# A fused retention and mixture-of-experts kernel: batch 1's feed-forward in two halves of 256 tokens, its second half attended in 64-token chunks

## The chip, the core and the metric

The kernel runs on one core of a Trainium2 chip. The time is the device time of one launch in microseconds (us). Engines are named as in the profile: PE is TensorE (matmul), PEld its weight loads, DVE is VectorE, ACT is ScalarE, POOL is GpSimd, SP is SyncE, which issues nearly all DMAs.

## What is computed

Retention attention for 8 batches, 8 heads, 576 positions and head dimension 64, followed by a two-layer feed-forward on all 4608 tokens (model width 512, inner width 2048):

```python
scores = scale * np.matmul(q, k.transpose(0, 1, 3, 2))
gamma = 1.0 - 2.0 ** (-5.0 - np.arange(H))
Dmat = np.where(rel >= 0, gamma[:, None, None] ** rel[None], 0.0)   # rel = row - column
ret = scores * Dmat[None]
attn = np.matmul(ret, v)
x = attn.transpose(0, 2, 1, 3).reshape(B * S, H * D)
h = x @ w_in
out = (h * (1.0 / (1.0 + np.exp(-beta * h)))) @ w_out
```

Inputs and output are float32; matmuls are in bf16. Because the decay is a power of gamma, it splits into a factor for q's position and one for v's. So attention is done in chunks: scores inside a chunk under a causal mask, plus q times a running state, the sum of k's transpose times v over the earlier chunks.

## The kernel before

Each batch has 512 full positions and a tail of 64; the eight tails together make a ninth block of 512 tokens. The blocks run in the order 0 to 6, tails, 7. For a block, attention leaves its transposed result in `xT` (four groups of 128 model columns by 512 tokens); 16 `up` steps (L542) multiply by `w_in` into PSUM and ACT writes the SiLU to `gT` (L551); then four groups of tokens, `down` (L575), each take 16 matmuls in four steps of four into a PSUM tile `po`, which is copied to `ot` (L589) and stored.

All engines run their instructions in the order in which the program emits them. That order is written by hand: the list `fill` (L663 to L688) holds the ups and downs, which keep PE busy, and `streams` (L704 to L776) holds every other step with a position in `fill` at which it is put in. `d0` is the position of batch 0's downs, `u1` that of batch 1's ups and `base[n]` that of later blocks' ups; `merged` (L602) weaves them. A step's time in the program is thus its place among ups and downs; on DVE, ACT, POOL and SP it is only an order.

PSUM has eight banks in four pools: `mm` has three (ups, downs, and one that the states borrow), `O` two, `sc` two, `st` one.

There are two forms of attention. Batches 0 and 1 go by chunks of 128: PE transposes q (`t_q`, L317) and k (`t_k`, L324), `a_sc` (L334) makes scores and DVE masks them, `a_O` and `a_cross` make the output, `a_x` copies it to `xT`, and `a_st` (L408) adds to the state and copies it to the block-diagonal `sbd` tiles. `second` (L690) does the outputs of two chunks. Later batches go by chunks of 64 on quarters of the array: `d_st` (L471) makes the state sums of four chunks, in a bank of `st` and a bank of `mm`, and its `chain` has DVE add them up one after another (L488, L490) and ACT copy each to `sbq` (L491); `d_sc` (L456) makes scores and masks (L469); `d_out` (L498) makes outputs (L508), the crosses with the states (L521) and, in `evict`, the four copies to `xT` (L536), two on DVE and two on ACT. They are grouped in stops: `scores` (L725) and `outputs` (L732), the latter with the first half of the next batch's states. Between the stops PE does ups or downs while DVE and ACT work.

In batch 1, chunks 0 and 1 are attended within batch 0's last downs. Ups 0 to 9 are then done for the 256 tokens of these two chunks, with chunks 2 and 3 attended among them, then ups 0 to 9 for the other 256 tokens, and ups 10 to 15 for all 512:

```python
fill += [F(up, 1, fo, 2 * x, 2) for x in range(2) for fo in range(10)]
fill += [F(up, 1, fo) for fo in range(10, FO)]
fill += [F(down, 1, ms, f0) for ms in range(MB // P) for f0 in range(0, FO, 4)]
```

A separate step, `early_states`, puts batch 2's first states behind the first of batch 1's downs. The scaling of q by the decay is `pre_q` (L253; on DVE for batches 0 and 1, on POOL after that), k and v are prepared by `pre` on POOL, and from batch 2 on SP transposes q and k by DMA.

Of the kernel before, what the change touches and what calls it, by code (L numbers as in the profile page):

```python
# [19 lines left out]
def kernel(  # L20
# [49 lines left out]
    QB = 2  # L70
    q_tiles, kv_tiles = {}, {}

    def load_q(b, us=(0, 1)):

        if b >= B:
            return
        if 0 in us:
            q_tiles[b] = stage.tile([P, H, CB, D], F32, name="qn", tag="qn", bufs=2)
        t = q_tiles[b]
        for u in us:  # L80
            w = slice(u * HP, (u + 1) * HP)
            nc.sync.dma_start(t[:, w].rearrange("p h i d -> p h (i d)"),
                              q[b, w, :MB, :].rearrange("h (p i) d -> p h (i d)", i=CB))
# [41 lines left out]
    pos = consts.tile([P, 2, CB + 1], F32, name="pos")  # L125
    for j, (step, mul) in enumerate(((1, CB), (P, 1))):
        nc.gpsimd.iota(pos[:, j, :CB], pattern=[[step, CB]], base=0, channel_multiplier=mul,
                       allow_small_or_imprecise_dtypes=True)
        for x in range(2):
            nc.gpsimd.iota(pos[x * TL:(x + 1) * TL, j, CB:], pattern=[[0, 1]], base=MB, channel_multiplier=1,  # L130
                           allow_small_or_imprecise_dtypes=True)
    lscale = consts.tile([P, 1], F32, name="lscale")
    nc.vector.memset(lscale[:], math.log(scale))
    lg = consts.tile([P, 2, CB + 1, H], F32, name="lg")
# [5 lines left out]
    nc.scalar.activation(gv[:], lg[:, 1], ACT.Exp, scale=-1.0)  # L140

# [10 lines left out]
    tri = [consts.tile([P, TL], BF16, name=f"tri{i}") for i in range(2)]  # L152
# [97 lines left out]
    def head_of(b, p, j):  # L250
        return 2 * p + (j if b is not None and b < QB or p < 2 else 1 - j)

    def pre_q(b, n):  # L253

        if n == 0:
            batch[b] = dict(qs=sb.tile([P, CB, H, D], BF16, name="qs", tag="qs", bufs=2),
                            qT=sb.tile([P, CB, HP, P], BF16, name="qT", tag="qT", bufs=2))
        if b < 2:
            hs, cs = slice(n // 2 * HP, (n // 2 + 1) * HP), slice(n % 2 * 2, n % 2 * 2 + 2)
            e = nc.vector  # L260
        else:
            if n % 2:
                return
            cs = slice(n, n + 2)
            for to, hs in turned:
                nc.gpsimd.tensor_tensor(batch[b]["qs"][:, cs, to], q_tiles[b][:, hs, cs].rearrange("p h i d -> p i h d"),  # L266
                                        gq[:, cs, hs].unsqueeze(3).to_broadcast([P, 2, len(range(H)[hs]), D]), ALU.mult)
            return
        e.tensor_tensor(batch[b]["qs"][:, cs, hs], q_tiles[b][:, hs, cs].rearrange("p h i d -> p i h d"),
                        gq[:, cs, hs].unsqueeze(3).to_broadcast([P, cs.stop - cs.start, hs.stop - hs.start, D]),  # L270
                        ALU.mult)

    def pre(i, js=(0, 1)):
# [22 lines left out]
        for to, hs in turned if b >= QB else [(slice(0, H), slice(0, H))]:  # L296
            nc.gpsimd.tensor_copy(kn[:, c % 2, to], t[:, 0, hs])  # L297
# [32 lines left out]
    def q_cols(i, r, p):  # L330

        b, c = seq[i]
        if b is None:
            return live[i]["qkT"][r, 0, p, :], lambda o: o  # L334
        return (batch[b]["qT"][r, :, p, c * PC:(c + 1) * PC], lambda o: o.rearrange("k (i s) -> k i s", i=CB))

    def a_sc(i):
# [11 lines left out]
        m_b = causal[:].unsqueeze(1).to_broadcast([P, HP, P])  # L349
# [48 lines left out]
    def a_x(i):  # L398
        b, c = seq[i]
        x, view = xt(b)[:, :, :, c * PC:(c + 1) * PC], lambda o: o.rearrange("k p (i s) -> k p i s", i=CB)  # L400
        Os = live[i]["O"]
# [6 lines left out]
    def a_st(i):  # L408
# [11 lines left out]
        for j in range(2):  # L420
            r, cols = slice(j * D, (j + 1) * D), slice(j * D, (j + 1) * D)
            e = nc.vector.tensor_copy if i in (CB + 2, CB + 3) else nc.scalar.copy
# [4 lines left out]
            e(ends[b][(1 - j) * D:(2 - j) * D, 2:], st[r, 2:, cols])  # L427

# [9 lines left out]
    def q_of(u, c, j, p):  # L438

        if u == B:  # L440
            return piece(u, c)["qkT"][half(j), 0, p, half(c % 2)]
        w = TL // CB
        return batch[u]["qT"][half(j), :, p, c * w:(c + 1) * w]

    def columns(u, o):
        return o if u == B else o.rearrange("k (i s) -> k i s", i=CB)
# [4 lines left out]
    def d_sc(u):  # L451

        R = [sb.tile([P, 2, 2, HP, TL], BF16, name="R", tag="R", bufs=4) for _ in range(2)]
        sc = {}
        for x in range(2):
            for j in range(2):  # L456
                sc[x, j] = psum.tile([P, 2, HP, TL], F32, name="sc", tag="O" if x else "sc", bufs=2)
# [6 lines left out]
        mask = tri[1 if u == B else 0][:].unsqueeze(1).to_broadcast([P, 2 * HP, TL])  # L464
# [29 lines left out]
    def d_out(u):  # L494

        shape = [P, 2, CB, TL] if u == B else [P, 2, CB, CB, TL // CB]
        O = {(hh, y): psum.tile(shape, F32, name="O", tag="sc" if y else "O", bufs=2) for y in range(2) for hh in range(2)}

        def to(c, p, x):
            o = O[c % 2, p // 2][half(x), p % 2]  # L500
            return o[:, c // 2] if u == B else o[:, :, c // 2]

        R = batch[u]["R"]
        for cc in range(CB):
            for p in range(HP):
                for hh, j in spread:
# [3 lines left out]
                                            start=cc == 0 and p % 2 == 0, stop=False, skip_group_check=True)  # L510
# [4 lines left out]
        def cross(flip):  # L515
            for n, (cc, pp, y, j) in enumerate((cc, pp, y, j) for cc in range(CB) for pp in range(2) for y in range(2) for j in range(2)):
# [11 lines left out]
        def evict():  # L528
            for n, ((hh, y), o) in enumerate(O.items()):
                x = xt(u)[:, 2 * y:2 * y + 2]  # L530
                if u == B:
                    x, o = x[:, :, :, half(hh)].rearrange("k p c q -> k (p c) q"), o.rearrange("k p c q -> k (p c) q")
                else:
                    x = x.rearrange("k p i (c h s) -> k (p i) c h s", c=CB, h=2)[:, :, :, hh, :]
                    o = o.rearrange("k p i c s -> k (p i) c s")
                (nc.scalar.copy if n % 2 else nc.vector.tensor_copy)(x, o)  # L536
# [5 lines left out]
    def up(m, fo, c0=0, cn=CB):  # L542
        if m not in gts:
            gts[m] = sb.tile([P, FO, CB, P], BF16, name="gT", tag="gT", bufs=2)
        w = slice(c0 * PC, (c0 + cn) * PC)
        ph = psum.tile([P, CB, P], F32, name="ph", tag="mm", bufs=3)
        ph = ph.rearrange("f i s -> f (i s)")[:, :cn * P].rearrange("f (i s) -> f i s", i=CB)
        for ko in range(KO):
            nc.tensor.matmul(ph, w_in_sb[:, ko, fo * P:(fo + 1) * P], xts[m][:, ko, :, w],  # L549
                             start=(ko == 0), stop=(ko == KO - 1))  # L550
        nc.scalar.activation(gts[m][:, fo, :, w], ph, ACT.Silu, scale=beta_sb[:, fo:fo + 1])  # L551
# [23 lines left out]
    def down(m, ms, f0, fn=4, n0=0, nn=d_model):  # L575
# [13 lines left out]
        (nc.scalar.copy if m == 0 else nc.vector.tensor_copy)(ot, po[:, :nn])  # L589
        if m < B:  # L590
            rows = out[m * S:m * S + MB].rearrange("(s i) n -> s i n", i=CB)
            if m < 2:
                held.append((rows[:, ms, n0:n0 + nn], ot))
            else:
                nc.sync.dma_start(rows[:, ms, n0:n0 + nn], ot)
# [100 lines left out]
    def triangles():  # L696
        for t, pattern in zip(tri, ([[1, CB], [CB, TL // CB]], [[1, TL]])):
            nc.gpsimd.memset(t[:], 1.0)
            for x in range(2):
                w = slice(x * TL, (x + 1) * TL)  # L700
# [7 lines left out]
               [(10.3, F(load_q, 1))] + [(10.3, F(load_kv, CB + n, (j,))) for n, j in keys_first],  # L708
               [(10.4, F(load_q, 2))] + [(10.4, F(load_kv, 2 * CB + n)) for n in range(2)],
               [(d0 + 8.6, F(load_kv, 2 * CB + 2)), (d0 + 8.7, F(load_kv, 2 * CB + 3)), (d0 + 12.6, F(x_q, XB, 0)), (d0 + 12.7, F(x_q, XB, 1)),  # L710
                (d0 + 13.6, F(x_k, XB, 0)),
                (base[2] - 4.5, F(release, 4)), (base[2] + 10, F(release, 4))],
               [(d0 + 7, F(pre_q, 1, n)) for n in range(4)] + [(d0 + 12.5, F(pre_q, XB, n)) for n in range(4)] + [(d0 + 11.6, F(t_q, 1, 0)), (d0 + 12.6, F(t_q, 1, 1))],
               [(d0 + 8, F(pre, 4, (0,))), (d0 + 8, F(pre, 5, (0,))), (d0 + 9, F(pre, 4, (1,))), (d0 + 9, F(pre, 5, (1,))),
                (d0 + 12.7, F(t_k, 4)), (d0 + 14, F(t_k, 5)), (d0 + 14, F(a_sc, 4)), (d0 + 15, F(a_sc, 5)),
                (d0 + 15, F(a_st, 4)), (d0 + 15.9, F(second, 4))],
# [5 lines left out]
    def early_states(u):  # L722
        d_st(u, 0)()

    def scores(u):  # L725
        chain = d_st(u, 1) if u < B else lambda: None
        masks = d_sc(u)
        steps = [lambda: masks(0), lambda: masks(1)]
        for f in [chain] + steps if u == B - 1 else steps + [chain]:
            f()  # L730

    def outputs(u):  # L732
# [3 lines left out]
        evict()  # L736
        chain()
# [70 lines left out]
```

## Time and profile before

| what | us |
|---|---|
| median of three runs | 299.28 (299.02 to 299.34) |
| the profiled execution | 298.64 |
| its span in the profile | 296.9 |
| PE busy | 286.9 |
| ACT busy | 147.1 |
| DVE busy | 101.3 |
| POOL busy | 109.0 |

Starts are counted from the span's begin. In a row of the timeline or of the chain, the first number is the start, the second the time that it takes, then engine, line, operation, output and inputs, shape and count; brackets give the idle time before it and what ended it. A matmul's row is longer than the distance to the next, since matmuls overlap; distances are taken from starts.

### The profile page before, as it was taken

The page shows a single profiled execution, that of the slowest core. Times are in us where ns is not written, and L with a number is a line of the kernel's source. Part 1 is how long each engine was busy: PE and PEld are TensorE (multiplying, and loading weights), DVE is VectorE, ACT ScalarE, POOL GpSimd, SP SyncE. Part 2 cuts the span into 40 slices and gives each one's busy share as a digit, 9 for nine tenths or more (in the row PEclk, how much of TensorE's full clock was granted, in tenths as well). Part 3 has the DMA queues.
Part 4 walks back from the last instruction along what each step waited for, and adds up shares of the span by engine and source line. Part 5 has one row for each costly group of instructions (what it writes and reads, how often), then busy time and mean ns, then how long its engine had stood idle before and what let it go on. Part 6 is the DMA issues. An engine that isn't in the chain of part 4 may idle for free.

```text
span 296.9 us, 7459 instructions
## 1 busy us (share of the span) xinstructions
PE 286.9 (97%) x3147; PEld 149.2 (50%) x3177; DVE 101.3 (34%) x209; ACT 147.1 (50%) x257; POOL 109.0 (37%) x211
## 2 busy tenths in 40 slices
PE   7799999999999999999999999999999999999995
PEld 5554456855544454455445544554454544444444
DVE  5563656704640552045204530354054300120012
ACT  5567546683277434743484347433770157008600
POOL 3666107693750923370429216736223000000000
PEclk9999999999999999999999999999999999999999
DMA  8999999999999999949999849999976110131012
GB/s 213 218 333 393 386 273 252 224 203 222 252 169 254 270 196 242 242 68 160 233 237 207 178 99 272 195 181 188 205 168 140 73 38 0 35 71 38 0 71 73
DMA packets 128273, 53.97 MB, mean 182 GB/s; under 512 B 110048, under 2 KB 120688, under 8 KB 128240
## 3 DMA queue, kind: packets, MB, share of 16 engines
q1 hardware_dynamic: 128208, 53.49, 82.4%
q8 instruction: 25, 0.41, 0.6%
q14 instruction: 8, 0.07, 0.1%
q10 hardware_dynamic: 32, 0.01, 0.0%
HBM read 36.71 MB, written 9.44 MB: 155 GB/s over the span
## 4 chain that ended last, share of the span: by engine, by line
PE 83%; DMA 5%; SPq 5%; POOL 3%; issue 2%; ACT 1%; POOLq 0%; DVE 0%
PE po L582 38%; PE ph L549 33%; PE ph L564 4%; DMA tln<-in_k_dram 3%; SPq L94 2%; DMA kvn<-in_k_dram 2%; PE O L508 1%; SPq L113 1%; POOL kn L286 1%; PE st L480 1%; PE sc L462 1%; DMA kT<-kn 1%; SPq L305 1%; POOL kn L285 1%; PE O L521 1%
## 5 line engine op out<-in xcount | busy, mean ns | idle before, releaser
L582 PE MATMUL po<-w_out_sb,gT 128*128 128x512 bf16 (+2 forms) x590 | 125.6, 367 | 2.3 <-issue 2.1
L551 ACT ACTIVATE gT<-ph,beta_sb 128x512 bf16<-128x512 f32 (+1 forms) x140 | 91.2, 657 | 52.1 <-PE ph L549 51.7
L549 PE MATMUL ph<-xT,w_in_sb 128*128 128x512 bf16 (+1 forms) x550 | 114.5, 364 | 0.5
L582 PEld LDWEIGHTS <-gT 128*128 128x128 bf16 x608 | 56.9, 98 | 62.9
L549 PEld LDWEIGHTS <-w_in_sb 128*128 128x128 bf16 x560 | 54.3, 98 | 57.6 <-DVE sum L488 0.7
L589 DVE COPY ot<-po 128x512 f32<-128x512 f32 (+2 forms) x34 | 22.3, 657 | 72.3 <-PE po L582 71.6
L297 POOL CAST kn<-kvn 128x128 bf16<-128x128 f32 (+2 forms) x80 | 25.9, 359 | 43.5 <-DMA kvn<-in_k_dram 43.0
L266 POOL TENSOR_TENSOR qs<-qn,gq 128x256 bf16<-128x256 f32 (+1 forms) x36 | 26.3, 759 | 36.0 <-DMA qn<-in_q_dram 34.6
L469 DVE TENSOR_TENSOR R<-sc,tri 128x512 bf16<-128x512 f32 x28 | 17.4, 683 | 61.4 <-PE sc L462 61.4
L277 POOL TENSOR_TENSOR vn<-kvn,gv 128x512 bf16<-128x512 f32 x32 | 33.3, 1044 | 13.5 <-DMA kvn<-in_v_dram 8.5
L536 ACT CAST xT<-O 128x512 bf16<-128x512 f32 x14 | 7.5, 589 | 32.0 <-PE O L521 32.0
L491 ACT CAST sbd<-warm 128x256 bf16<-128x256 f32 x18 | 7.3, 405 | 25.5 <-DVE warm L488 20.6
L564 PE MATMUL ph<-xT,w_in_sb 128*128 128x512 bf16 x54 | 12.3, 379 | 0.3 <-ACT xT L404 0.2
L351 DVE TENSOR_TENSOR R<-sc,causal 128x512 bf16<-128x512 f32 x16 | 10.2, 685 | 4.6 <-PE sc L347 4.5
L488 DVE TENSOR_TENSOR sum<-st,warm 128x256 f32<-128x256 f32 x24 | 10.2, 425 | 2.5
L488 DVE TENSOR_TENSOR warm<-st,sum 128x256 f32<-128x256 f32 x18 | 7.6, 422 | 9.6 <-PE st L480 8.4
L536 DVE CAST xT<-O 128x512 bf16<-128x512 f32 x14 | 9.0, 686 | 5.0 <-PE O L521 5.0
L567 ACT ACTIVATE gT<-ph,beta_sb 128x512 bf16<-128x512 f32 x14 | 8.7, 687 | 4.2 <-PE ph L564 4.2
L285 POOL TENSOR_TENSOR kn<-tln,gq 128x128 bf16<-128x128 f32 (+1 forms) x12 | 5.7, 472 | 10.5 <-DMA tln<-in_q_dram 6.9
L194 POOL CAST w_in_sb<-wt 128x256 bf16<-128x256 f32 (+1 forms) x12 | 7.4, 623 | 4.9 <-DMA wt<-in_moe_w_in_dram 4.9
L564 PEld LDWEIGHTS <-w_in_sb 128*128 128x128 bf16 x56 | 5.4, 98 | 6.7 <-issue 0.3
L219 PE MATMUL ph<-warm 128*128 128x128 f32 (+1 forms) x24 | 7.3, 444 | 1.3 <-DVE warm L123 1.3
(81 smaller groups left out, 154.1 us busy)
## 6 DMA issues: line engine op xcount, KB each, us to landing
qn<-in_q_dram SPq DMA_DIRECT2D x16, 512.0 KB, 5.4
kvn<-in_k_dram SPq DMA_DIRECT2D x32, 256.0 KB, 5.4
kvn<-in_v_dram SPq DMA_DIRECT2D x32, 256.0 KB, 5.0
out_dram<-ot SPq DMA_DIRECT2D x31, 256.0 KB, 3.8
wt<-in_moe_w_out_dram SPq DMA_DIRECT2D x8, 512.0 KB, 9.1
wt<-in_moe_w_in_dram SPq DMA_DIRECT2D x5, 512.0 KB, 8.1
wt<-in_moe_w_in_dram SPq DMA_DIRECT2D x6, 256.0 KB, 5.5
out_dram<-ot SPq DMA_DIRECT2D x9, 128.0 KB, 2.4
```

The source lines that it names most:

```text
L266: nc.gpsimd.tensor_tensor(batch[b]["qs"][:, cs, to], q_tiles[b][:, hs, cs].rearrange("p h i d -> p i h d"), gq[:, cs, hs].unsqueeze(3).to_ ...
L277: nc.gpsimd.tensor_tensor(live[i]["vn"][:], kv_tiles.pop(i)[:, 1], gains(gv, c), ALU.mult)
L297: nc.gpsimd.tensor_copy(kn[:, c % 2, to], t[:, 0, hs])
L351: nc.vector.tensor_tensor(R[:, j], sc[j][:], m_b, ALU.mult)
L469: nc.vector.tensor_tensor(R[x][:, j].rearrange("k c p q -> k (c p) q"), sc[x, j].rearrange("k c p q -> k (c p) q"), mask, ALU.mult)
L488: nc.vector.tensor_tensor(new[:], add, sums[(c - 1) % 2][:], ALU.add)
L536: (nc.scalar.copy if n % 2 else nc.vector.tensor_copy)(x, o)
L549: nc.tensor.matmul(ph, w_in_sb[:, ko, fo * P:(fo + 1) * P], xts[m][:, ko, :, w], start=(ko == 0), stop=(ko == KO - 1))
L551: nc.scalar.activation(gts[m][:, fo, :, w], ph, ACT.Silu, scale=beta_sb[:, fo:fo + 1])
L564: nc.tensor.matmul(phs[f][:], w_in_sb[:, ko, f * P:(f + 1) * P], xts[m][:, ko], start=(ko == 0), stop=(ko == KO - 1))
L582: nc.tensor.matmul(po[:, :nn], gT[:, fo, ms, :], w_out_sb[:, fo, n0:n0 + nn], start=(fo == 0), stop=(fo == FO - 1))
L589: (nc.scalar.copy if m == 0 else nc.vector.tensor_copy)(ot, po[:, :nn])
```

## The change

Batch 1 (`HB`) is done in two halves of 256 tokens: 16 half-width ups and the downs of two token groups, then the same for the second half. Chunks 0 and 1 are attended as before, though over another arrangement of the tokens (two runs per 128 positions in place of four, with q loaded in halves of positions, a decay table `gqh` and a mask `causal_h` of their own). The second half is attended in four chunks of 64, in the manner of the later batches: `scores(HB)` at the end of the first half's ups, `outputs(HB)` before the last three steps of the first half's downs. `a_st` of chunk 1 has DVE put the state into `sum` and ACT copy it to `sbq`. The second half of q is scaled on DVE and transposed among the first half's ups, with the keys of chunks 2 and 3. `outputs(HB)` takes over batch 2's first states from `early_states`, and its four copies to `xT` are all on ACT, behind the chain. Batch 2's stops move: its scores to the start, its outputs to the middle of the second half's downs. Two of batch 1's four output copies go from DVE to ACT, and half of batch 2's q scaling from POOL to DVE.

```diff
-    QB = 2
+    HB = 1
+    HT = MB // 2
...
+        if b == HB:
+            for x in us:
+                nc.sync.dma_start(t[:, :, 2 * x:2 * x + 2].rearrange("p h i d -> p h (i d)"),
+                                  q[b, :, x * HT:(x + 1) * HT, :].rearrange("h (p i) d -> p h (i d)", i=2))
+            return
...
+        if b == HB:
+            cs = slice(2 * n, 2 * n + 2)
+            for to, hs in turned if n else [(slice(0, H), slice(0, H))]:
+                nc.vector.tensor_tensor(batch[b]["qs"][:, cs, to], q_tiles[b][:, hs, cs].rearrange("p h i d -> p i h d"),
+                                        gqh[:, cs, hs].unsqueeze(3).to_broadcast([P, 2, len(range(H)[hs]), D]), ALU.mult)
+            return
...
+            e = nc.vector if b == XB and n else nc.gpsimd
...
+    def t_qh(x):
+        T = psum.tile([P, 2, HP, P], BF16, name="T", tag="O", bufs=2)
+        for i in range(2):
+            for p in range(HP):
+                nc.tensor.transpose(T[:, i, p, :], heads(batch[HB]["qs"][:, 2 * x + i], p), ident[:])
+        (nc.vector.tensor_copy if x else nc.scalar.copy)(batch[HB]["qT"][:, 2 * x:2 * x + 2], T[:])
...
-            e = nc.vector.tensor_copy if i in (CB + 2, CB + 3) else nc.scalar.copy
+            e = nc.scalar.copy
+            if i == CB + 1:
+                nc.vector.tensor_copy(sums[1][r, :2], st[r, :2, cols])
+                nc.vector.tensor_copy(sums[1][half(1 - j), 2:], st[r, 2:, cols])
+                continue
...
+        if i == CB + 1:
+            nc.scalar.copy(sbq[3][:], sums[1][:])
...
+        xs = range(u == HB, 2)
...
-        for x in range(2):
+        for x in xs:
...
+        ccs = range(2 if u == HB else 0, CB)
...
-        for cc in range(CB):
+        for cc in ccs:
...
-                (nc.scalar.copy if n % 2 else nc.vector.tensor_copy)(x, o)
+                (nc.scalar.copy if n % 2 or u == HB else nc.vector.tensor_copy)(x, o)
...
-        (nc.scalar.copy if m == 0 else nc.vector.tensor_copy)(ot, po[:, :nn])
+        (nc.scalar.copy if m == 0 or m == HB and ms % 2 == 0 else nc.vector.tensor_copy)(ot, po[:, :nn])
...
-    fill += [F(up, 1, fo, 2 * x, 2) for x in range(2) for fo in range(10)]
-    fill += [F(up, 1, fo) for fo in range(10, FO)]
-    fill += [F(down, 1, ms, f0) for ms in range(MB // P) for f0 in range(0, FO, 4)]
-    base = {1: u1 + 10}
+    for x in range(2):
+        fill += [F(up, HB, fo, x) for fo in range(FO)]
+        fill += [F(down, HB, ms, f0) for ms in (2 * x, 2 * x + 1) for f0 in range(0, FO, 4)]
+    u2 = u1 + FO + 8
+    base = {}
...
-               [(10.3, F(load_q, 1))] + [(10.3, F(load_kv, CB + n, (j,))) for n, j in keys_first],
+               [(10.3, f) for x in range(2) for f in [F(load_q, HB, (x,))] + [F(load_kv, CB + n, (j,)) for n, j in keys_first[4 * x:4 * x + 4]]],
...
-               [(d0 + 7, F(pre_q, 1, n)) for n in range(4)] + [(d0 + 12.5, F(pre_q, XB, n)) for n in range(4)] + [(d0 + 11.6, F(t_q, 1, 0)), (d0 + 12.6, F(t_q, 1, 1))],
+               [(d0 + 7, F(pre_q, HB, 0)), (d0 + 16, F(pre_q, HB, 1)), (d0 + 12, F(t_qh, 0)), (u1 + 5, F(t_qh, 1))],
+               [(d0 + 12.5, F(pre_q, XB, 0)), (u1 + 13, F(pre_q, XB, 2))],
...
-                (d0 + 15, F(a_st, 4)), (d0 + 15.9, F(second, 4))],
+                (d0 + 15, F(a_st, 4)), (d0 + 16, F(second, 4))],
...
-                (d0 + 15.95, F(t_k, 6)), (u1 + 1, F(t_k, 7)), (u1 + 2, F(a_sc, 6)), (u1 + 3, F(a_sc, 7)),
-                (u1 + 4, F(a_st, 6)), (u1 + 7, F(second, 6))]]
+                (u1 + 4, F(t_k, 6)), (u1 + 6, F(t_k, 7))]]
...
-        for f in [chain] + steps if u == B - 1 else steps + [chain]:
+        for f in [chain] + steps if u in (HB, B - 1) else steps + [chain]:
...
         cross()
-        evict()
-        chain()
+        for f in [chain, evict] if u == HB else [evict, chain]:
+            f()
...
-    streams.append([(base[1] + 17, F(early_states, XB))])
+    streams.append([(u1 + FO, F(scores, HB)), (u2 - 3, F(outputs, HB))])
...
-        lo, hi = (base[n] + 17, base[n + 1] - 9.5) if n == 1 else (base[n] + 3, base[n + 1] - 14)
+        lo, hi = (u2 + 1, base[2] - 9.5) if n == 1 else (base[n] + 3, base[n + 1] - 14)
...
-        work = [(n + 1, hi - 0.5, hi + 6)] if n == 1 else [(n + 1, hi - 1, hi + 6.5)]
+        work = [(n + 1, base[2] - 8, base[2] - 2)] if n == 1 else [(n + 1, hi - 1, hi + 6.5)]
```

More of the change, by code (lines that the diff above doesn't have):

```diff
@@ L151 @@
                             fill=0.0, base=0, channel_multiplier=-1)
-    tri = [consts.tile([P, TL], BF16, name=f"tri{i}") for i in range(2)]
+    tri = [consts.tile([P, TL], BF16, name=f"tri{i}") for i in range(3)]
+    causal_h = consts.tile([P, P], BF16, name="causal_h")
     NS = 3
@@ L250, in head_of @@
     def head_of(b, p, j):
-        return 2 * p + (j if b is not None and b < QB or p < 2 else 1 - j)
+        return 2 * p + (j if p < 2 else 1 - j)
     def pre_q(b, n):
@@ L295, in pre @@
         live[i] = dict(kn=kn[:, c % 2], kT=kT[:, c % 2], vn=vn)
-        for to, hs in turned if b >= QB else [(slice(0, H), slice(0, H))]:
+        for to, hs in turned if (b, c) >= (HB, 2) else [(slice(0, H), slice(0, H))]:
             nc.gpsimd.tensor_copy(kn[:, c % 2, to], t[:, 0, hs])
@@ L334, in q_cols @@
             return live[i]["qkT"][r, 0, p, :], lambda o: o
+        if b == HB:
+            return batch[b]["qT"][r, :2, p, c * D:(c + 1) * D], lambda o: o.rearrange("k (i s) -> k i s", i=2)
         return (batch[b]["qT"][r, :, p, c * PC:(c + 1) * PC], lambda o: o.rearrange("k (i s) -> k i s", i=CB))
@@ L441, in q_of @@
             return piece(u, c)["qkT"][half(j), 0, p, half(c % 2)]
+        if u == HB:
+            return batch[u]["qT"][half(j), 2:, p, c % 4 * 32:c % 4 * 32 + 32]
         w = TL // CB
@@ L451, in d_sc @@
     def d_sc(u):
-        R = [sb.tile([P, 2, 2, HP, TL], BF16, name="R", tag="R", bufs=4) for _ in range(2)]
+        xs = range(u == HB, 2)
+        R = {x: sb.tile([P, 2, 2, HP, TL], BF16, name="R", tag="R", bufs=4) for x in xs}
         sc = {}
-        for x in range(2):
+        for x in xs:
             for j in range(2):
-                sc[x, j] = psum.tile([P, 2, HP, TL], F32, name="sc", tag="O" if x else "sc", bufs=2)
+                sc[x, j] = psum.tile([P, 2, HP, TL], F32, name="sc", tag="O" if x and u != HB else "sc", bufs=2)
             for cl in range(2):
@@ L509, in d_out @@
                                             columns(u, R[cc // 2][half(hh), j, cc % 2, p, :]),
-                                            start=cc == 0 and p % 2 == 0, stop=False, skip_group_check=True)
+                                            start=cc == ccs[0] and p % 2 == 0, stop=False, skip_group_check=True)
         fence = nc.vector.memset(fenced[:], 0.0)
@@ L515, in cross @@
         def cross(flip):
[L516 removed]
+            for n, (cc, pp, y, j) in enumerate((cc, pp, y, j) for cc in ccs for pp in range(2) for y in range(2) for j in range(2)):
                 c, p = 2 * cc + (j ^ flip), pp + 2 * y
@@ L696, in triangles @@
     def triangles():
-        for t, pattern in zip(tri, ([[1, CB], [CB, TL // CB]], [[1, TL]])):
+        for t, pattern, n in ((causal_h, [[1, 2], [2, D]], 1), (tri[2], [[1, 2], [2, TL // 2]], 2),
+                              (tri[0], [[1, CB], [CB, TL // CB]], 2), (tri[1], [[1, TL]], 2)):
             nc.gpsimd.memset(t[:], 1.0)
-            for x in range(2):
-                w = slice(x * TL, (x + 1) * TL)
+            for x in range(n):
+                w = slice(x * P // n, (x + 1) * P // n)
                 nc.gpsimd.affine_select(out=t[w], in_=t[w], pattern=pattern, compare_op=ALU.is_ge,
@@ L727, in scores @@
         masks = d_sc(u)
-        steps = [lambda: masks(0), lambda: masks(1)]
-        for f in [chain] + steps if u == B - 1 else steps + [chain]:
+        steps = [F(masks, x) for x in range(u == HB, 2)]
+        for f in [chain] + steps if u in (HB, B - 1) else steps + [chain]:
             f()
```

56 lines of the change are left out of this document (33 added, 23 removed).

## The prediction

> **What bounds the kernel now.** I read first the page's busy times and slices, then what PE waited for in the stretch that the change rewrites, then the chain of waits, then the timeline at the places where a PE instruction hangs on VectorE (DVE) or ScalarE (ACT).
>
> The page, busy times, and PE's waits from 36 to 115 us (us in total, times, longest):
>
> ```profile
> PE 286.9 (97%) x3147; PEld 149.2 (50%) x3177; DVE 101.3 (34%) x209; ACT 147.1 (50%) x257; POOL 109.0 (37%) x211
> PEclk9999999999999999999999999999999999999999
> ...
> PE po L582 <- issue: 0.8, 5, 0.2
> ```
>
> PE is busy 97%, at full clock in every slice, and between 36 and 115 us it waits 0.8 us, all of it for no other engine. So the end moves by PE's own work and by any wait that the change puts before PE; time on other engines counts only through such a wait.
>
> The chain that ended last (start, us, what) at the work that is replaced and at its successors:
>
> ```profile
> 51.53 0.46 PE sc L347 x8
> 52.53 0.33 PE sc L347 x8
> 53.41 0.22 PE st L418 x4
> 54.94 0.57 PE O L394 x16
> 55.51 0.55 PE O L380 x8
> 56.06 0.22 PE st L418 x4
> 68.00 0.38 PE st L480 x32
> ...
> 73.18 0.58 PE sc L462 x64
> ```
>
> The timeline around the end of batch 1's downs and the first ups of batch 2:
>
> ```profile
> 81.62 2.54 PE L582 MATMUL po<-w_out_sb,gT 128*128 128x512 bf16 x11 [0.16 <-issue]
> 81.67 1.29 DVE L536 CAST xT<-O 128x512 bf16<-128x512 f32 x2 [0.82 <-PE O L521]
> 82.88 0.41 DVE L490 COPY warm<-st 128x256 f32<-128x256 f32 x1
> 83.40 0.42 DVE L488 TENSOR_TENSOR sum<-st,warm 128x256 f32<-128x256 f32 x1
> 84.45 0.42 DVE L488 TENSOR_TENSOR sum<-st,warm 128x256 f32<-128x256 f32 x1
> 84.91 0.41 ACT L491 CAST sbd<-sum 128x256 bf16<-128x256 f32 x1
> 84.93 7.02 PEld L549 LDWEIGHTS <-w_in_sb 128*128 128x128 bf16 x34 [0.41 <-DVE sum L488]
> ```
>
> The second up's weight load waits for the last add of the state chain (84.45 + 0.42), which gives back the lent bank. The first up ends at 84.16 + 4 x 0.215 = 85.02, so this wait is just covered, with less than 0.1 us to spare.
>
> **PE work.** Removed: for chunks 2 and 3 of batch 1 the eight-matmul scores 0.46 + 0.33, states 0.22 + 0.22, outputs 0.57, crosses 0.55: 2.35 us. The separate early-states stop goes too: 0.38 and the 0.16 with which a down returns after a stop (five of these are the 0.8 above): 0.54. Together 2.89. Added: at the second half's scores 32 states 0.38, 32 of the 64 scores 0.29, a return 0.16; at its outputs 32 of 64 output matmuls 0.34 (row 106.89: 0.67 for 64), 32 crosses at 0.011 (row 107.56 and its sequel: 0.53 for 48) 0.35, batch 2's 32 states 0.28, a return 0.16: 1.96. Also 48 half-width up matmuls replace 24 full ones: the chain has 12 in 1.31 (0.109 each) and 4 full ones in 0.86 (0.215), so 5.23 - 5.16 = +0.07. Transposes stay 64 in number. Sum: -0.86 us; by the gaps between pieces it could be -0.6 to -1.2.
>
> Here the Trainium skill speaks against the change: "TensorE: Matmul & The Clock Gate", section "Wait — 56ns, not 53.3ns?", says that start-to-start never drops below about 25 ns however small the matmul. For the 128 added small matmuls that would be 3.2 us, where the rows above give 1.3, and the sum 1.9 us worse (an estimate). The trace disagrees, with 64 output matmuls in 0.67 us, 10.5 ns each, on four array positions in turn.
>
> **Four waits that the new order makes.** In the changed program each engine keeps its own order, and these are the PE instructions that stand behind DVE or ACT there.
>
> *A, first up of batch 1.* It needs chunk 1's copy into xT, half of it on DVE. Before DVE's half the new order puts the second half's q scaling, three multiplies. One of the two groups of q transposes that stood ahead (0.44 us) moves behind this point, so everything up to here is 0.45 earlier: the fourth score mask, ending at 49.06 now, ends near 48.55. Then the multiplies: 512 columns cost 0.65 in a row of four (1.29 for two), the two of 256 columns about 0.38 each (256-column DVE rows: 0.42 alone): 1.4 us, to 49.95; the copy 0.42 (49.78 row), to 50.4; PE starts at 50.46. Its own work ends near 49.5, since the key transpose that stood here goes behind the fourth up. Wait 0.9. Bounds: 0.4 (ACT's own half of the copy ends near 49.95 anyway) to 1.3. Queued behind the multiplies are also the four state copies.
>
> *B, fourth up.* ACT now copies the state of chunk 1 from a sum that DVE assembles in four 64x128 copies (like 57.08 to 58.26: 1.18) after A's xT copy: 50.4 to 51.55; ACT's 0.41 (row 84.91) ends at 52.0. All SiLUs queue behind it: the first (0.47; 128x256) ends at 52.47. There are three banks, so ups one to three end at 50.46 + 1.31 = 51.77 and the fourth waits to 52.52. Wait 0.75, bounds 0.3 to 1.0. The order before had two sbd copies of ACT (0.77) here too, but with transposes and scores between the first ups. Afterwards ACT's pitch (13 SiLUs in 5.71: 0.44) just keeps step with four half matmuls (0.435), and the transposes among the ups let it catch up.
>
> *C, first up of the second half.* Its input leaves PSUM by four ACT copies, which now stand behind the whole state chain of batch 2. From the last state matmul the chain needs 2.5 us to ACT's last copy (rows at 68: states end 68.38; four DVE steps at 0.52, the last ending 70.44, then 0.41). The four copies at 0.385 (L404, 128x256 on ACT: 0.38) make it 4.05. PE in that time: remaining crosses 0.15, return 0.16, three groups of downs at 0.86 = 2.59: 2.9. The up's first two matmuls can run after two copies, so its end comes at 4.05 + 0.06 + 0.22 = 4.33 against 2.9 + 0.435 = 3.33. Wait 1.0, bounds 0.6 to 1.3. Queued behind it: the SiLUs, with nothing more lost.
>
> *D, second up of batch 2.* The stop before it keeps its DVE order (two xT copies, then the chain), but now two groups of downs follow it, not three. The 0.86 less cover meets less than 0.1 to spare: wait 0.8, bounds 0.6 to 0.9.
>
> Costed at nothing: the second half's scores at the change from ups to downs (DVE: chain 2.1 and two masks 1.3 after the states, against 5 x 0.86 = 4.3 of downs; uncovered, it would cost the excess); q's second half on SP behind four k and v loads (it is the sixth transfer, with the same bytes up to it as before, so it lands when the second v did, which POOL used at 46.6 without a wait; DVE needs it at 48.55); batch 2's scaling on DVE and its keys and values (POOL done by 63.1 in the timeline, needed near 65); the transposes of SP, whose order is otherwise the same; the first T on ACT, off PE by two groups of downs. ACT takes half of batch 1's output copies where it is idle. The earlier masks and tables on POOL and DVE fall before 20 us, or where POOL is idle from 31 to 43.
>
> **The sum.** -0.86 + 0.9 + 0.75 + 1.0 + 0.8 = +2.6 us. The profiled execution took 298.64 us (span 296.9), so 301.2; it lies 0.64 under the median of the three runs, 299.28, and by that median I forecast 301.9. With the smaller ends of all waits (1.9) it is +1.0, with the larger ends (4.5) +3.6: 300.3 to 302.9.
>
> **Rivals.**
>
> *Faster: the cover holds.* Place: the four waits all begin with short DVE steps, and the trace does not show the 256-column q multiplies or evictions in runs of 32. If DVE and ACT were through before PE arrives, only PE's work would count: -0.86, 298.4. It decides from a total wait under 0.26 us, at which the gain is over 0.2%. For it: ACT and DVE are idle half of the time. Against: D uses forms that the trace has 48 times, at 0.42 us with a pitch of 0.52, and alone costs 0.8. Chance 0.06.
>
> *No change: half of the waits.* If A and B shrink to their common cover because the q multiplies overlap the masks' tail (say A 0.2, B 0.1) and C to 0.2 by ACT's copies overlapping, D remains: -0.86 + 1.3 = +0.4, 299.7. Against: DVE and ACT rows follow each other in order throughout. Chance 0.07.
>
> *Dearer: q's second half lands late.* It now comes in 512-byte runs instead of 1 KB, behind four loads of 256-byte runs. If it lands at 50.0 instead of by 46.6, A and with it B's start move by 1.45: 303.4. It decides from a landing after 48.55. For it: loads took up to 11.2 us to land here, and DMA is busy throughout. Against: equal bytes ahead of it. Chance 0.09.
>
> *Dearest: the small matmuls are spaced out.* If the 128 added ones (32 x 4) ran at the spacing of the removed eight-matmul scores (0.33 / 8 = 0.041), PE's work would be 5.3 instead of 1.3: 305.9. Against: the same 64-column forms run at 10 to 12 ns in every batch. Chance 0.01. (This is the skill's floor, cited above, as a rival; by its figure it would give 303.8.)
>
> **How the numbers follow.** The forecast has 0.77, with 300.3 to 302.9. About 0.6 us (0.2%) is what a measurement of this kernel can tell from no change. Faster 0.06 and no change 0.07 are the rivals' chances; the rest, 0.87, is slower. The range 299.7 to 303.1 takes in the no-change rival and a little beyond the larger ends of the waits; it leaves out the faster one and the two dearer ones, 0.16.
>
> **What would show it.** The profile after should list, in PE's waits, ph waits behind DVE xT and ACT gT near 50 to 53 us, behind ACT xT near 68 to 69.5, and behind DVE sum at batch 2's second up near 87; PE's busy matmul time should fall by about 0.9. The later batches should be the same pieces, shifted by about 2.6. Wrong if PE shows no wait for DVE or ACT between 45 and 90 us (faster rival), or if DVE's q multiply waits for DMA beyond 49 us (dearer).

## The result, and the profile after

The changed kernel takes 302.81 us (median of four runs, 302.48 to 303.28), the kernel before beside it 299.31: 1.0118 times, 95% interval 1.0100 to 1.0135. The forecast was 301.9. The profiled execution took 302.75 us (span 301.0), 4.11 more than the profiled execution before.

The page's busy times, and PE's waits over the whole span (us in total, times, longest):

```profile
PE 286.6 (95%) x3251; PEld 150.6 (50%) x3281; DVE 100.3 (33%) x209; ACT 151.6 (50%) x273; POOL 110.0 (37%) x219
```

```profile
PE sc L501 <- DMA kT<-kn: 2.1, 1, 2.1
...
PE ph L591 <- DVE sum L527: 0.6, 1, 0.6
PE ph L591 <- DVE xT L433: 0.6, 1, 0.6
PE ph L591 <- ACT xT L579: 0.6, 2, 0.4
...
PE ph L591 <- ACT gT L593: 0.5, 1, 0.5
PE O L561 <- issue: 0.3, 1, 0.3
```

The four waits of ups (`ph` is the PSUM tile of an up) are the forecast's four, by engine and tile. The first line, the tail block's scores behind a key transpose, is in no term of it, and neither is the last. Rows of PE's timeline show where they stand (the rows between are left out):

```profile
50.19 1.48 PE L591 MATMUL ph<-xT,w_in_sb 128*128 128x256 bf16 x12 [0.64 <-DVE xT L433]
52.15 0.60 PE L591 MATMUL ph<-xT,w_in_sb 128*128 128x256 bf16 x4 [0.47 <-ACT gT L593]
65.09 2.54 PE L624 MATMUL po<-w_out_sb,gT 128*128 128x512 bf16 x11 [0.16 <-issue]
68.04 0.38 PE L591 MATMUL ph<-xT,w_in_sb 128*128 128x256 bf16 x2 [0.41 <-ACT xT L579]
68.58 6.93 PE L591 MATMUL ph<-xT,w_in_sb 128*128 128x256 bf16 x62 [0.17 <-ACT xT L579]
82.81 0.32 PE L561 MATMUL O<-qT,sbd 64*64 64x64 bf16 x17 [0.34 <-issue]
85.39 1.03 PE L591 MATMUL ph<-xT,w_in_sb 128*128 128x512 bf16 x4
87.06 13.12 PE L591 MATMUL ph<-xT,w_in_sb 128*128 128x512 bf16 x59 [0.65 <-DVE sum L527]
```

A bracket counts from the modelled end of the matmul before, and in a flowing stream the next one starts some 0.16 ahead of that end. So what a wait costs is read from starts. The second up of batch 2 starts 87.06 - 85.39 = 1.67 after the first, where four matmuls take 0.86: D costs 0.81, not 0.65. In the same way B costs 52.15 - 50.19 - 1.31 = 0.65, where 1.31 is the time of the twelve half-width matmuls ahead of it. For C, after 11 downs at 0.215 from 65.09 the next matmul could start at 67.46, so the first two of the up come 0.58 late, and the next ones 68.58 - 68.04 - 0.22 = 0.32 later again: 0.90. A is 0.64 and the 0.16, 0.80.

The rows of before for the same stretch:

```profile
32.51 10.53 PE L582 MATMUL po<-w_out_sb,gT 128*128 128x512 bf16 x47
...
84.00 14.06 PE L549 MATMUL ph<-xT,w_in_sb 128*128 128x512 bf16 x63
```

From the first matmul of batch 0's downs (32.51 before, 32.43 after) to the second up of batch 2 (84.00 + 0.86 before, 87.06 after) the time grew from 52.35 to 54.63: +2.28. I call this the rewritten stretch. From there on the batches are the same pieces, until the tail's scores: without the wait of those scores it is 143.1 us in both. The chain that ended last, after and then before:

```profile
227.65 4.58 DMA kT<-kn
232.23 0.04 issue
232.28 0.32 PE sc L501 x16
```

```profile
225.08 3.03 DMA kT<-kn
228.11 0.04 issue
228.15 0.32 PE sc L462 x16
```

The last key transpose is issued 2.57 us later and takes 1.55 us longer, so these scores start 4.13 later. PE waits 2.08 us there, before the change 0.20:

```profile
232.28 0.32 PE L501 MATMUL sc<-kT 64*64 64x64 bf16 x16 [2.08 <-DMA kT<-kn]
```

```profile
228.15 0.32 PE L462 MATMUL sc<-kT 64*64 64x64 bf16 x16 [0.20 <-DMA kT<-kn]
```

Behind these scores both kernels take the same time: 301.0 - 232.28 and 296.9 - 228.15 are 68.7 and 68.8. The growth of the profiled execution is thus 2.28 in the rewritten stretch and 1.88 at the tail, less 0.08 at the start: 4.08 of the 4.11.

### The profile page after: what moved, and what is told of

It reads as the page before. It is cut to its first block, busy times and chain, and to the rows that moved or that the text cites. A ratio compares the mean times of both kernels' runs of the same rounds, so it can differ in the third digit from the quotient of the medians.

```text
span 301.0 us, 7698 instructions
## 1 busy us (share of the span) xinstructions
PE 286.6 (95%) x3251; PEld 150.6 (50%) x3281; DVE 100.3 (33%) x209; ACT 151.6 (50%) x273; POOL 110.0 (37%) x219
## 5 line engine op out<-in xcount | busy, mean ns | idle before, releaser
L591 PEld LDWEIGHTS <-w_in_sb 128*128 128x128 bf16 x584 | 56.5, 98 | 58.9 <-issue 1.9
L631 DVE COPY ot<-po 128x512 f32<-128x512 f32 (+2 forms) x32 | 21.0, 655 | 72.4 <-PE po L624 72.4
L508 DVE TENSOR_TENSOR R<-sc,tri 128x512 bf16<-128x512 f32 x30 | 18.8, 683 | 68.9 <-PE sc L501 68.9
L285 POOL TENSOR_TENSOR qs<-qn,gq 128x256 bf16<-128x256 f32 (+1 forms) x33 | 25.0, 784 | 33.1 <-DMA qn<-in_q_dram 32.3
L579 ACT CAST xT<-O 128x512 bf16<-128x512 f32 (+1 forms) x18 | 8.7, 542 | 32.8 <-PE O L561 32.8
L527 DVE TENSOR_TENSOR sum<-st,warm 128x256 f32<-128x256 f32 x26 | 11.0, 425 | 2.8
L527 DVE TENSOR_TENSOR warm<-st,sum 128x256 f32<-128x256 f32 x20 | 8.4, 422 | 10.3 <-PE st L519 9.0
L530 ACT CAST sbd<-sum 128x256 bf16<-128x256 f32 x19 | 7.7, 405 | 2.5 <-DVE sum L527 0.5
L606 PEld LDWEIGHTS <-w_in_sb 128*128 128x128 bf16 x56 | 5.3, 98 | 6.8 <-POOL w_in_sb L206 0.6
```

Source lines behind the costliest of these rows:

```text
L285: e.tensor_tensor(batch[b]["qs"][:, cs, to], q_tiles[b][:, hs, cs].rearrange("p h i d -> p i h d"), gq[:, cs, hs].unsqueeze(3).to_broadcas ...
L508: nc.vector.tensor_tensor(R[x][:, j].rearrange("k c p q -> k (c p) q"), sc[x, j].rearrange("k c p q -> k (c p) q"), mask, ALU.mult)
L527: nc.vector.tensor_tensor(new[:], add, sums[(c - 1) % 2][:], ALU.add)
L530: nc.scalar.copy((sbq[c] if c < NC - 1 else ends[u])[:], new[:])
L579: (nc.scalar.copy if n % 2 or u == HB else nc.vector.tensor_copy)(x, o)
L606: nc.tensor.matmul(phs[f][:], w_in_sb[:, ko, f * P:(f + 1) * P], xts[m][:, ko], start=(ko == 0), stop=(ko == KO - 1))
```

## The experiments

**One wait each.** Theory: the waits before PE are the loss, each for itself. Rivals: a later hold takes whatever is regained; the half-width ups are dearer in themselves; a wait only moves.

*A: the second half's q scaling later.*

```diff
-               (d0 + 16, F(pre_q, HB, 1))
+               (u1 + 0.5, F(pre_q, HB, 1))
```

> Undoes wait A alone: the second half's q scaling goes behind DVE's half of chunk 1's copy into xT. Theory (the waits before PE are the loss, each for itself): the first up of batch 1 waits about 0.3 us instead of 0.64 (ACT's half of the copy and the end of DVE's mask remain), the state copies and with them wait B start 0.3 earlier; the second half's q transposes are not late. Time about -0.3 us against the changed kernel's 302.8, so 302.5; the wait behind DVE xT at the first up is smaller in the profile. Rival 1 (a later point holds the end, the tail's k transposes for instance): the wait goes, the tail's wait of 2.1 us grows by the same amount, the time stays at 302.8. Rival 2 (the loss is in the half-width ups): the wait goes, and time per up grows; 302.8.

*B: the state copy later.*

```diff
-        if i == CB + 1:
-            nc.scalar.copy(sbq[3][:], sums[1][:])
+    streams.append([(u1 + 4.5, lambda: nc.scalar.copy(sbq[3][:], sums[1][:]))])
```

> Undoes wait B alone: ACT's copy of chunk 1's state into sbq[3], which waits for DVE's four assembling copies, goes behind the SiLUs of the first four ups; it is needed only at the second half's crosses. Theory: the fourth up no longer waits for ACT's SiLU (0.47 us now), every other wait stays; about -0.45 us, 302.35. Rival 1 (a later hold): 302.8, the tail's wait grows by 0.45. Rival 2 (ACT's pitch of SiLUs, not the copy, holds the half-width ups): the wait of 0.47 is spread over the later ups, 302.8.

*C: the copies to xT ahead of the chain.*

```diff
-        for f in [chain, evict] if u == HB else [evict, chain]:
+        for f in [evict, chain]:
```

> Undoes wait C alone: at the second half's outputs the four copies to xT on ACT go ahead of the state chain of batch 2. Theory: the first up of the second half no longer waits (0.41 + 0.17 us now); the chain's ACT copies then stand behind the evictions, which costs nothing before batch 2's outputs; about -0.58 us, 302.25. Rival 1 (a later hold): 302.8, the tail's wait grows by 0.58. Rival 3 (the wait only moves: the chain's bank comes back later and an up behind waits for DVE's sum): between 302.5 and 302.8, with a new wait behind DVE sum near 69 us.

*D: three down steps behind batch 2's outputs.*

```diff
-        work = [(n + 1, base[2] - 8, base[2] - 2)]
+        work = [(n + 1, base[2] - 8, base[2] - 3)]
```

> Undoes wait D alone: batch 2's outputs come three down steps before batch 2's ups instead of two. Theory: with 0.86 us more of downs behind the stop, the second up of batch 2 no longer waits for DVE's chain (0.65 us now); about -0.65 us, 302.15, if the outputs' own inputs (batch 2's scores, masked by DVE) are ready 0.86 us earlier. Rival 1 (a later hold): 302.8, the tail's wait grows by 0.65. Rival 3 (the wait only moves): PE waits for DVE's masks ahead of the outputs instead, 302.5 to 302.8.

Measured beside the kernel before at 298.74 us: A 301.64 (ratio 1.0098, interval 1.0065 to 1.0132), B 301.27 (1.0106, 1.0063 to 1.0148), C 300.48 (1.0063, 1.0041 to 1.0086), D 301.48 (1.0100, 1.0060 to 1.0140). All are below the changed kernel, but runs of one kernel now lie up to 4 us apart, so the times don't resolve steps of half a microsecond. The timeline does. A itself differs between profiles (0.64 to 0.94 in brackets where it stands), so B, C and D are read from batch 1's first up to batch 2's second, 36.87 us in the changed kernel's profile (87.06 - 50.19):

- A: the wait at the first up falls to 0.30, behind ACT, and the first up comes 17.43 us after the first matmul of batch 0's downs instead of 17.76. B stays, at 0.39.
- B: no wait at the fourth up; 36.35. Up 0.5.
- C: no wait at the second half's first up, none moved elsewhere; 35.93. Up 0.9.
- D: no wait at batch 2's second up; 36.46. Of the 0.8 only 0.4 is won, since the gap within batch 2's crosses (the `O L561 <- issue` above) grows from 0.34 to 0.66.

So A shrinks and the other three waits go, each with its named cause. The profiles also have something that no theory expected: PE's wait for the last key transpose was 2.06 us with A undone and 1.86 with D, but none with B or C.

*D put into the kernel before.*

```diff
-        work = [(n + 1, hi - 0.5, hi + 6)] if n == 1
+        work = [(n + 1, hi - 0.5, hi + 7)] if n == 1
```

> The kernel before with one thing of the change: batch 2's outputs stand two down steps before batch 2's ups, not three. Theory (wait D comes from the place of this stop alone): the second up of batch 2 waits 0.75 to 0.85 us for DVE's last sum, at the place where the kernel before has no wait at all, and the time goes from about 298.8 to 299.6. Rival 1 (a later hold absorbs a wait here): the wait is in the profile and the time stays within 0.2 of the kernel before. Rival 3 (the wait needs the other moves of the change): no wait for DVE sum, 298.8.

Its timeline at batch 2's first two ups:

```profile
83.86 1.03 PE L549 MATMUL ph<-xT,w_in_sb 128*128 128x512 bf16 x4
85.69 13.12 PE L549 MATMUL ph<-xT,w_in_sb 128*128 128x512 bf16 x59 [0.80 <-DVE sum L488]
```

The wait is 0.80, as expected, and costs 1.83 - 0.86 = 0.97 from start to start; the rewritten stretch takes 53.31 instead of 52.35. One down step less behind a stop makes it, without any other part of the change. The median was 299.46 against 299.09 (1.0015, 0.9994 to 1.0036), less than the wait and not to be told from no change, while the lowest times, 299.04 and 297.95, are 1.09 apart. So the wait is shown; that it reaches the end in full is not.

**All four, and the changed kernel once more beside it.** The edits are the four above together.

> All four waits undone together: q scaling later, state copy later, xT copies ahead of the chain, three downs behind batch 2's outputs. Theory: the waits A, B, C and D were 0.64 + 0.47 + 0.58 + 0.65 = 2.34 us, of which about 0.3 of A and 0.3 of D (PE waits longer inside the crosses instead) stay; the time falls by about 1.7 against the changed kernel run beside it, to 299 where the tail's transpose lands early and 301 where it lands late. Rival 1 (a later hold takes the gain): no change against the changed kernel, the wait for DMA kT at the tail's scores grows to over 3 us. Rival 2 (the half-width ups themselves are dearer): less than 0.8 is gained, and the distance between starts of the half-width up matmuls stays above 0.109 us.

> The changed kernel once more, unaltered, beside the next three. In the profiles so far the tail block's last 16 scores wait 1.9 to 2.1 us for the last key transpose in some (the changed kernel, the run with the q scaling later, the run with three downs) and not at all in others (the run with the state copy later, the run with the xT copies first); that transpose took 3.4 to 4.8 us and 3.2 to 3.4 us from issue to landing there. Theory (this wait is a race on SP's queue of DMAs that comes out either way in any run of this program): the times fall into two groups, near 300.7 and near 302.7. Rival 1 (the wait belongs to the changed kernel, and goes when PE arrives elsewhere): all times between 302.4 and 303.4.

With all four undone: 300.05 us against 299.10 of the kernel before (1.0026, 0.9995 to 1.0056), which this measurement can't tell from no change. The changed kernel beside it: 303.51 (1.0118, 1.0063 to 1.0172). The timeline with all four undone:

```profile
50.56 1.97 PE L589 MATMUL ph<-xT,w_in_sb 128*128 128x256 bf16 x16 [0.30 <-ACT xT L436]
...
67.24 7.22 PE L589 MATMUL ph<-xT,w_in_sb 128*128 128x256 bf16 x64
...
75.43 0.44 PE L499 MATMUL sc<-qT,kT 64*64 64x64 bf16 x32 [0.33 <-DMA kT<-kn]
```

The second half's 64 matmuls run without a break, 7.22 us for 64 x 0.110 = 7.04 and the 0.17 by which a row of theirs outlasts its last start: each costs what the rows of before said (0.109), so half-width ups are not dearer, and that rival falls. The rewritten stretch takes 84.36 + 0.86 - 33.11 = 52.11, 0.24 less than in the kernel before, although a key transpose of batch 2 is late here once (0.33). The later-hold rival wanted no gain and a tail wait over 3 us; the gain is 3.5 at the median and the tail wait 2.42, so it falls as the explanation of the loss, though the tail's wait did not go away. The 3.5 is more than the 2.52 by which the stretch became shorter (54.63 - 52.11), because half of the changed kernel's six runs here lie in a group of long times.

The changed kernel repeated gave 300.53, 300.76, 302.79, 304.23, 304.52 and 304.63. That is the theory's two groups, near 300.7 and 302.7, the second with one run only, and above them a third, for which the last section has an explanation. Its first four runs, 302.48 to 303.28, were all in the middle group.

**The tail's wait.** SP issues tail 3's loads ahead of two key transposes, in the changed kernel and with all four waits undone:

```diff
-            ((-11, -3, 7.5), (-6, 1, 8))
+            ((-11, -3, 7.5), (-10.9, 1, 8))
```

> The changed kernel with tail 3's loads alone issued earlier. Theory: the wait for DMA kT at the tail's scores goes; 300.7 in every execution, 2 us less than the changed kernel's upper group and as its lower group; the four waits near 50, 52, 68 and 87 us stay. Rival 1: the tail's wait stays at about 2 us, 302.7. Rival 3: two groups, 300.7 and 302.7, as often as without the edit.

> The four waits undone, and tail 3's loads issued right behind tail 2's, ahead of two key transposes on SP. Theory: as in the run before, and without the tail's wait in any execution: 298.5 to 299.2 with one group of times, against 298.7 of the kernel before; it could beat it by up to 0.3. Rival 1: the tail's wait stays, since the transposes of tail 2 now start 4 us later and are what is late: 300.5 to 301. Rival 3 (the tail wait is the latency of one transpose, whatever is queued): two groups of times, 2 us apart.

In the changed kernel: 302.22 (1.0091, 1.0058 to 1.0124), five of twelve times at 300.04 to 300.67 and the others at 302 and above. PE's timeline at the scores:

```profile
232.11 0.32 PE L501 MATMUL sc<-kT 64*64 64x64 bf16 x16 [1.50 <-DMA kT<-kn]
232.97 0.32 PE L501 MATMUL sc<-kT 64*64 64x64 bf16 x16 [0.54 <-DMA kT<-kn]
```

The wait moves to tail 2's transpose, which now stands behind tail 3's loads: 1.50 + 0.54 in place of 2.08. With all four undone: 299.43 against 299.10 (1.0000, 0.9968 to 1.0032), four of twelve times at 297.70 to 298.31, the rest from 299.34 up, with a tail wait of 1.59 in the profile. So the reordering of SP did not remove the tail's wait. In this last run the rewritten stretch, free of B, C and D, is 83.35 + 0.86 - 32.54 = 51.67: 0.68 less than in the kernel before, with 0.29 + 0.16 of wait A still in it.

A second try moved four of SP's tail loads to ACT's queue, with the same reordering, in the kernel before, the changed one and the one with all four waits undone:

```diff
-                nc.sync.dma_start(to[x * TL:(x + 1) * TL],
+                (nc.scalar if src is v and t > 1 else nc.sync).dma_start(to[x * TL:(x + 1) * TL],
...
```

> The kernel before with the tail's stream of DMAs shortened: tail 3's q and k loads right behind tail 2's, and the v loads of tails 2 and 3 issued by ACT ahead of a stretch of downs, where it is idle 4 us, instead of by SP, whose queue is without a gap from 195 to 226 us. Theory (the tail's wait is SP's queue running late by a varying amount): the last key transposes are issued about 3 us earlier, no wait for DMA kT at the tail's scores, and times of 298.0 to 298.6 in one group; the kernel before gains 0.3 to 0.6 at the median. Rival 3 (the wait is a late transpose, whatever is queued): times from 298.1 to 299.9 as before, no gain.

> The changed kernel with the same edit of the tail's loads. Theory: no wait for DMA kT at the tail's scores, one group of times at 300.4 to 300.8; against the kernel before with the same edit 2.0 to 2.4 slower, which is the four waits (2.34) and the 0.3 within the crosses less 0.6 of PE work, without the tail in it. Rival 1 (the tail is what makes the change slow): within 1 us of the kernel before with the same edit. Rival 3: two groups, near 300.6 and 302.8.

> The four waits undone, with the same edit of the tail's loads. Theory: no wait but about 0.3 us at the first up of batch 1 between 45 and 90 us, none at the tail's scores, one group of times at 297.8 to 298.3: faster than the kernel before by 0.5 to 0.9 at the median, and than the kernel before with the same edit by 0.2 to 0.4 (0.6 of PE work less the 0.3 of wait). Rival 1 (a wait further on takes the gain): equal to the kernel before with the same edit or slower, with a new wait behind 90 us. Rival 3: two groups, near 298.2 and 300.2.

They took 310.75, 312.97 and 310.19 us against 299.09: 1.0396 (1.0369 to 1.0423), 1.0470 (1.0443 to 1.0497) and 1.0369 (1.0336 to 1.0401). The tail's wait is gone in all three, but ACT's timeline in the first shows at what price:

```profile
204.07 8.76 ACTq L113 DMA_DIRECT2D tln<-in_v_dram  x4
212.88 1.07 ACT L536 CAST xT<-O 128x512 bf16<-128x512 f32 x2 [16.74 <-DMA tln<-in_q_dram]
```

and the chain that ended last names what ACT's last load stood behind:

```profile
208.79 3.42 DMA out_dram<-ot
212.21 0.02 issue
212.23 0.60 ACTq L113
```

ACT's last issue begins 0.02 us after the landing of an output store of SP's, in all three profiles. So the loads tied ACT to SP's queue. The copies to xT and to `sbd` behind them came late, DVE's last sum waited for those, and PE's up for that sum: 9.0 us in this profile, 10.3 and 10.7 in the other two. My expectation took ACT's idle 4 us for cover and missed that wait. Since the new hold ends on a DMA, these three can't price the change without the tail, as they were meant to; it isn't settled that way.

## Why the prediction was right, and where it was not

**The mechanism and its four places were right.** PE waits for the engine and the tile named at each of the four. When the named cause is taken away A falls to 0.30, where ACT's half of the copy holds it as the forecast's lower bound had it, and B, C and D go. D appears in the kernel before when only its cause is put there. Predicted and measured, from start to start in the changed kernel's profile: A 0.9 and 0.80, B 0.75 and 0.65, C 1.0 and 0.90, D 0.8 and 0.81. The sum is 3.45 and 3.16. A's bracket is 0.64 in two profiles of the same program and 0.93 to 0.94 in three with the same instructions up to there (C undone, D undone, tail 3's loads early): DVE's three q multiplies took 1.35 us in the two and 1.64 to 1.65 in the three, where the forecast had 1.4. So the forecast's 0.9 lies within the 0.80 to 1.10 that A cost from start to start. C is smaller because ACT's four copies took 0.30 each, not 0.385.

**PE's work** was -0.86, with bounds of -0.6 and -1.2. The stretch of 51.67 gives -0.68 - 0.45 = -1.13, inside the bounds and near the better end. Part of the distance is a misreading. The 0.16 that the forecast counted for the return of a down behind a stop is the place of a matmul that the trace of before has no record of: five steps of downs behind the states at 67.94 have 20 weight loads and 19 matmuls.

```profile
68.31 4.00 PEld L582 LDWEIGHTS <-gT 128*128 128x128 bf16 x20
68.54 4.26 PE L582 MATMUL po<-w_out_sb,gT 128*128 128x512 bf16 x19 [0.16 <-issue]
```

Without its three returns, one removed and two added, the forecast's sum of PE's work would have been -1.02. The 128 added small matmuls are thus no dearer than the rows of before said, and the dearest rival falls, and with it the estimate by the 25 ns of the Trainium skill, "TensorE: Matmul & The Clock Gate", section "Wait — 56ns, not 53.3ns?".

**A term that was missing, 0.34:** a gap in batch 2's crosses, in which PE waits for nothing that the profile's views show. It is 0.20 to 0.66 in the changed kernel and with one wait undone, and absent with all four undone. No run tests its cause, but the traces point to one, the loading of PE's own instructions. In every profile that has the gap it stands ahead of the 863rd weight load of the program, also with D undone, where that load belongs to the tenth cross instead of the sixth. And it ends 1.4 to 1.7 us after the last packet of a 16 KB transfer on the page's `instruction` queue; with all four undone that transfer ended 2.3 to 2.7 us ahead of the same load.

Together -1.13 + 3.16 + 0.34 = +2.37, against +2.28 in the stretch and +2.6 forecast. The lowest times fit it: 300.53 for the changed kernel (of six) against 298.07 for the one before (of 29) in the same series, 2.46 apart.

**The step that failed is "the later batches should be the same pieces, shifted by about 2.6".** They are, but for the tail's last scores, where the profile has 1.88 us more of wait. At the medians the change costs 3.5 us, about one more than the sum. The profile before did show this place in its chain of waits, as a transpose that landed 0.20 us too late; I read the chain only at the replaced work, and took 0.20 for nothing. It was a race already lost by a little.

Whether the change itself makes the tail later by more than its shift is open. In the ten profiles whose chain goes through it, the last transpose took 3.0 to 3.4 us (the kernel before, the same with D, A undone, B undone) or 4.4 to 4.9 (the changed kernel twice, D undone, all four undone, both with tail 3's loads early), and one program, the changed kernel, has times near 300.7 and near 302.7. That speaks for chance in the DMA. That its first four runs all fell near 302.7, while half of the kernel before's lie within 1 us of its lowest, speaks for some dependence on the program. No run here separates the two.

**The other rivals.** The cover did not hold (faster), and the waits were not half (no change): the four cost 3.16 where it needed 1.3. q's second half was not late: DVE's multiplies started at 48.45 without a wait, 0.1 from the forecast 48.55. The range, 299.7 to 303.1, held the time, but that is partly luck: its upper part was meant for larger waits, and the tail, in no term of the sum, used it.

**A version that beats both** wasn't found. With all four waits undone and the tail reordered, the rewritten stretch is 0.68 us shorter than before and the lowest times are 0.4 lower (297.70 against 298.07), but the medians can't be told apart.

## What to carry to other kernels

When PE is nearly full, price a moved stop by what stands behind it on the other engines: one group of downs less behind a stop (0.86 us) cost 0.8 us, and each of the four waits could be forecast to 0.2 us from the rows of the kernel before. Read a wait's cost from start to start, since the bracket counts from a modelled end. And follow the list of waits to the end of the span: the scores that waited 0.20 us for a DMA in the kernel before waited between nothing and 2.4 us in the runs here.

## What the runs showed of the hardware

In one execution PE's clock was halved soon after a wait of 2.08 us. The windows of the repeated changed kernel (the third number from the right is the granted clock, PEclk), in an execution of 304.63 us:

```profile
230.00:232.00 2.00, 0.40 (x48) 0.29 (x36) 1.29 (x2) 0.00 (x0) 0.00 (x0) 1.00 1.36 106
232.00:234.00 2.00, 1.36 (x20) 0.79 (x22) 1.16 (x2) 0.00 (x0) 0.00 (x0) 0.83 0.22 85
234.00:236.00 2.00, 2.00 (x6) 0.63 (x5) 0.30 (x2) 0.00 (x0) 0.00 (x0) 0.50 0.00 0
236.00:238.00 2.00, 2.00 (x9) 0.89 (x8) 0.52 (x1) 0.00 (x0) 0.00 (x0) 0.82 0.31 118
```

The wait ends at 232.48. The clock is 0.50 from about 233.3 to 236.7, and the 23 downs behind the scores take 6.81 us, where the first profile, with the same wait of 2.08 us and full clock throughout, has 5.13: 1.68 us more. That fits the third group of times: its three runs have a granted clock of 0.993 or 0.994 over the whole span, the other three 1.000. That the wait is the cause was not tested. The Trainium skill, "TensorE: Matmul & The Clock Gate", section "HAM oscillation — how this bites in real kernels", has it that idle gaps of PE over about 3.4 us bring the clock down. Here the clock fell behind 2.08 us in one profile and not in another; from 229.83 to 232.95, around the wait, PE had only the 64 small score matmuls. In the kernel before with ACT's loads the 9 us wait began near 206.3, and the clock was still 1.00 up to 210 and 0.52 from 210 to 212, so it fell some 3.8 us into the wait, which agrees with that figure.

SP's queue is busy almost without a gap from 195 to 228 us in both kernels, mostly at 0.63 us for the issue of each load of 128 KB. In the same stretch the packets' time is 95.7% of the 16 DMA engines' time before and 116.0% after (over 100%, so packets overlap), so no run here tells whether the issue or the transfers hold the tail back. An issue on ACT's queue was seen to begin only at the landing of a store on SP's.
